# A fused retention and MLP kernel: half products in the second block, another order of plain units, and k scaled on GpSimd by a product

## The chip, the core and the metric

The kernel runs on one core of a Trainium2 chip. The metric is the device time in microseconds of one execution. The time before is the median of three runs, 205.53 us (205.35 to 206.09).

## What is computed

The reference is a retention layer (a decaying linear attention) over 4 batches, 8 heads, 768 tokens and a head size of 64, and behind it an MLP with a Mish-like gate over the 3072 tokens:

```python
gamma = 1.0 - 2.0 ** (-5.0 - np.arange(H))
for t in range(S):
    state = gamma * state + outer(k[t], v[t])
    y[t] = (1 / sqrt(D)) * q[t] @ state
x = y as (3072 tokens, 512)
h = x @ w_in                       # 512 -> 2048
g = h * tanh(log1p(exp(h)))        # Mish
out = g @ w_out                    # 2048 -> 512
```

Inputs and output are float32; the kernel multiplies in float16.

## The kernel before

The 3072 tokens are 24 chunks of 128, six to a batch. Chunks go in blocks: block 0 has four, blocks 1 to 10 two each. For each chunk q, k and v are loaded (a DMA each on SyncE's queue), scaled and cast to float16 (`casts`, L313 to L327), q and k are transposed by a DMA (`turn_by_dma`, L329) or on TensorE (`turn`, L354, for chunks 4 and 5), and then come the scores (L371), the mask (L377, VectorE), the state update (L385; su on VectorE at L397, st on GpSimd or VectorE at L398), y (L404 and L414) and the copy of y to xt (L460, ScalarE). In `casts` GpSimd makes three operations a chunk from chunk 6 on: q times a column of factors for each head (L319), k times one constant (L324, `tensor_scalar`), and v times a column of factors (L325). For chunks up to 5 ScalarE scales k (L322).

Everything is put in order by hand: the scheduler is manual, each engine works through its instructions in the order in which the program issues them, and each waits on semaphores for its inputs and for tiles to come free. For the first two blocks that order stands in `plan` dictionaries keyed by a unit number u; for the later blocks it stands in `steps_of`, keyed by step names ("p2", "p6", "p7", "p4", "h2", "end" in the first GEMM, "m2", "m7", "m3" in the second).

The two GEMMs of the MLP come in two forms:
- Plain. In blocks 0 and 1 `g1` (L468) makes the first GEMM: each unit fills one PSUM tile with matmuls against `win` (L475), and `mish` follows on ScalarE (L491). `g2_mm` (L495, L497) makes the second GEMM, 16 matmuls of 512 columns a chunk, and `g2_out` (L501) copies the result on VectorE (L503).
- With half products, from block 2 (`SEVEN = 2`). Matrices are cut in 2 x 2, and a product of two such matrices takes seven block products in place of eight, with sums of the inputs made beforehand and sums of the outputs behind. `g1_seven` (L578) does it for one half of the first GEMM's outputs: seven block products of eight 128-column matmuls (L600), with snapshots of PSUM on ScalarE (`snap`, L607) and sums on VectorE (`plus`, L617); the other half is made in four `plain` units of eight 256-column matmuls each (L620, L624, mish at L628). `seven` (L670) does it for the whole second GEMM: seven products of eight 256-column matmuls (L690), in the order a11 b11, a12 b21, s2 t2, s1 t1, s3 t3, s4 b22, a22 t4.

The sums that they need: `win_sums` (L546, written wsum, L562) and `weight_sums` (L511, written tmat, L527 to L530) once; `x_sums` (L569, xsum) of a block's xt before its first GEMM; and for the second GEMM sums of g in `gsum`: s1 and s2 by `sums_a` (L540, rows L543 and L544), s3 by `sums_b` (L664), s4 by `sums_c` (L668). All of them are VectorE operations on float16 tiles in SBUF. s1 is a21 + a22 and s2 is s1 - a11, so s2 of some f needs g of the units that made these f in all of those quarters. The 16 row blocks of g lie as f 0 to 7 in the first half and f 0 to 7 in the second; f 0 to 3 come from the half products, f 4 and 5 from `plain(1, 0)` and `plain(3, 0)`, f 6 and 7 from `plain(1, 1)` and `plain(3, 1)`.

Before the change the plain units stand in the order (1,0), (1,1), (3,0), (3,1), and `sums_a` is called twice, for f 0 to 3 at step "p7" and for f 4 to 7 at "end", behind the first mask of "h2". In block 1, the plain form, the eight tmat sums are issued one a unit (`extra`).

Of the kernel before, what the change touches and what calls it, by code (L numbers as in the profile page):

```python
# [9 lines left out]
FP16 = mybir.dt.float16  # L10
FP32 = mybir.dt.float32
AF = mybir.ActivationFunctionType
ALU = mybir.AluOpType
# [3 lines left out]
def kernel(  # L17
# [9 lines left out]
    nc = tc.nc  # L27
    B, H, S, D = q.shape
    d_model, d_ff = moe_w_in.shape
    P = 128  # L30
# [4 lines left out]
    TB = 512  # L35
    CPB = TB // C
# [4 lines left out]
    NFB = d_ff // P  # L41
    NBP = d_model // P
    NSL = 4
    FPS = NFB // NSL
# [36 lines left out]
    ident = cpool.tile([P, P], FP16, name="ident")  # L81
    tri = cpool.tile([P, C], FP32, name="tri")
    gcm = cpool.tile([P, HP, P], FP32, name="gcm")
    warm = cpool.tile([P, 1], FP32, name="warm")
    nc.gpsimd.memset(ident, 0.0)
    nc.gpsimd.affine_select(
# [17 lines left out]
    for h in range(H):  # L104
        o = 64 * (h % 2)
        nc.vector.memset(gcm[o:o + 64, h // 2, o:o + 64], float(gamma[h] ** C))

    win_ap = moe_w_in.rearrange("(bp p) f -> p bp f", p=P)
    wout_ap = moe_w_out.rearrange("(fb p) c -> p fb c", p=P)
# [5 lines left out]
    gtiles, tmats, gsums = {}, [], []  # L115
    wsums, hsnaps, tsums = [], [], {}
    nsnap = [0]
    SEVEN = 2
    nload, ncast = [0], [0]
    stores = []  # L120


# [190 lines left out]
    def casts(g):  # L313
        qf, kf, vf = loaded.pop(g)
        qk16 = castp.tile([P, 2, H, D], FP16, name="qk16")
        q16, k16 = qk16[:, 0], qk16[:, 1]
        v16 = castp.tile([P, H, D], FP16, name="v16")
        if qf is not None:
            nc.gpsimd.tensor_tensor(  # L319
                q16, qf, qs.unsqueeze(2).broadcast_to((P, H, D)), op=ALU.mult)  # L320
        if g < CPB + 2:
            nc.scalar.mul(k16, kf, BOOST)  # L322
        else:
            nc.gpsimd.tensor_scalar(k16, kf, BOOST, None, op0=ALU.mult)  # L324
        nc.gpsimd.tensor_tensor(  # L325
            v16, vf, vs.unsqueeze(2).broadcast_to((P, H, D)), op=ALU.mult)
        cast[g] = (q16, k16, v16, qk16)  # L327
# [170 lines left out]
            o_ps, gts[blk, fb][:, t * P:(t + 1) * P], wouts[s][:, f, cols],  # L498
            start=(fb == 0), stop=(fb == NFB - 1))

    def g2_out(o_ps, blk, t, due, cols=slice(None)):  # L501
        osb = op.tile(list(o_ps.shape), FP32, name="osb", tag="osb")
        nc.vector.tensor_copy(osb, o_ps)  # L503
        row0 = (first[blk] + t) * P
        dst = out[row0:row0 + P, cols]
        stores.append((due, dst, osb))
# [4 lines left out]
    def weight_sums(half):  # L511
        n, hf = NFB // 2, d_model // 2
        if half == 0:
            tmats.extend(
                wstage.tile([P, 2, n, hf], FP16, name="tmat", tag="wt", bufs=4)
                for _ in range(2))
            gsums.append(wstage.tile([P, 4, n, P], FP16, name="gsum", tag="wt", bufs=4))
            gsums.append(gp.tile([P, 4, n, P], FP16, name="gsum", tag="g0"))
            hsnaps.append(gp.tile([P, 4, TB], FP32, name="hsnap", tag="g0"))
        f = slice(half * FPS, (half + 1) * FPS)  # L520
        t1, t2 = tmats[0][:, 0, f], tmats[0][:, 1, f]
        t3, t4 = tmats[1][:, 0, f], tmats[1][:, 1, f]
        b11, b12 = wouts[half][:, :, :hf], wouts[half][:, :, hf:]
        b21, b22 = wouts[half + 2][:, :, :hf], wouts[half + 2][:, :, hf:]
        sub = ALU.subtract
        return [
            lambda: nc.vector.tensor_tensor(t1, b12, b11, op=sub),  # L527
            lambda: nc.vector.tensor_tensor(t2, b22, t1, op=sub),
            lambda: nc.vector.tensor_tensor(t3, b22, b12, op=sub),
            lambda: nc.vector.tensor_tensor(t4, b21, t2, op=sub),  # L530
        ]

    def sum_views(blk, f=slice(None)):
        s = gsums[blk % 2]
        n = NFB // 2
        lo, hi = gtiles[blk, 0][:, :n][:, f], gtiles[blk, 0][:, n:][:, f]
        return ([s[:, i, f] for i in range(4)],
                lo[:, :, :P], hi[:, :, :P], lo[:, :, P:], hi[:, :, P:])

    def sums_a(blk, half):  # L540
        n = NFB // 4
        (s1, s2, _, _), a11, _, a21, a22 = sum_views(blk, slice(half * n, (half + 1) * n))
        nc.vector.tensor_tensor(s1, a21, a22, op=ALU.add)  # L543
        nc.vector.tensor_tensor(s2, s1, a11, op=ALU.subtract)  # L544

# [32 lines left out]
    def g1_seven(blk, steps):  # L578
# [41 lines left out]
        def plain(s, half):  # L620
            h_ps = mmps.tile([P, 2, 2 * P], FP32, name="h_ps", tag="mm")
            for j in range(2):
                for bp in range(NBP):
                    nc.tensor.matmul(  # L624
                        h_ps[:, j], win(s, 2 * half + j, bp), xt(blk, bp),
                        start=bp == 0, stop=bp == NBP - 1)
            fb = s * FPS + 2 * half
            nc.scalar.activation(gt[:, fb:fb + 2], h_ps, AF.Mish, scale=inv_boost3)  # L628
# [21 lines left out]
        mish_of(1, 1, c22)  # L650
        mish_of(0, 1, c12)
        step("p7")
        plain(1, 1)
        mm(px, a(1, 1), t(4))
        mish_of(1, 0, px)
        step("p4")
        plain(3, 0)
        step("h2")
        plain(3, 1)
        step("end")  # L660
# [105 lines left out]
    def first_block():  # L766
# [85 lines left out]
            31: [(y_two, 1)],  # L852
        }
        o_tiles = [None] * CPB
        extra = []
        for u in range(2, 2 * NFB):
            if u < NFB:
                g1(0, u)
            elif u < 2 * NFB - 2:
                w = u - NFB  # L860
                for t in range(CPB):
                    if w == 0:
                        o_tiles[t] = mmps.tile([P, d_model], FP32, name="o_ps", tag="mm")
                    g2_mm(o_tiles[t], 0, t, w)
            else:
                for t in range(CPB // 2) if u % 2 == 0 else range(CPB // 2, CPB):
                    for w in range(NFB - 2, NFB):
                        g2_mm(o_tiles[t], 0, t, w)
                    g2_out(o_tiles[t], 0, t, 1)
            for fn, *args in plan.get(u + 1, ()):  # L870
                fn(*args)
            if u == NFB + 1:
                extra = win_sums()
            if extra:
                extra.pop(0)()

    def next_chunk(g):
        if g < NCK:
# [11 lines left out]
    def state_next(blk, j):  # L890
        if not last_of_batch(first[blk] + j):
            state(first[blk] + j, nc.gpsimd)

    def steps_of(blk):
        a, nb = first[blk] + 4, blk + 1
        ahead = nb < len(BLOCKS)

        def only(*work):
            return list(work) if ahead else []
        return {  # L900
            "p2": only((outer_next, nb), (state_next, nb, 0)),
            "p6": [(cast_to, a + 1), (next_chunk, a), (store_due, 1)],
            "p7": [(store_due, 2), *only((state_next, nb, 1)), (sums_a, blk, 0)],
            "p4": [(store_due, 3)],
            "h2": only((scores, a - 2), (scores, a - 1), (mask, a - 2)),
            "end": [(sums_a, blk, 1), (cast_to, a + 2), (next_chunk, a + 1)],
            "m2": only((mask, a - 1)),
            "m7": only((y_two, nb)),
            "m3": only((x_sums, nb)),
        }  # L910

    def plan_of(blk):
        a = first[blk] + 4
        early, then_seven = blk == 1, blk + 1 == SEVEN
        plan = {1: [(cast_to, a + 1)],
                (1 if early else 2 if then_seven else 4): [(cast_to, a + 1), (next_chunk, a)],
                (5 if early else 8): [(cast_to, a + 2), (next_chunk, a + 1)]}
        plan[10 if early else 7] = [(scores_two, blk + 1)]
        plan[12 if early else 10] = [(outer_two, blk + 1)]
        plan[14 if early else 13] = [(y_two, blk + 1)]  # L920
        return plan

    first_block()
    for blk in range(1, len(BLOCKS)):
        if blk >= SEVEN:
            steps = steps_of(blk)
            g1_seven(blk, steps)
            seven(blk, steps, blk + 1 == len(BLOCKS))
            continue
        n1 = NFB * BLOCKS[blk] // CPB  # L930
        plan = plan_of(blk)
        extra = []
        if blk + 1 == SEVEN:
            extra = weight_sums(0) + weight_sums(1)
        for u in range(2 * n1):
            store_due(u)
            if u < n1:
                g1(blk, u)
            else:
                t, part = divmod(u - n1, 4)  # L940
                if part == 0:
                    o_ps = mmps.tile([P, d_model], FP32, name="o_ps", tag="mm")
                for fb in range(part * 4, part * 4 + 4):
                    g2_mm(o_ps, blk, t, fb)
                if part == 3:
                    g2_out(o_ps, blk, t, u + 3 if t == 0 else 3)
            for fn, *args in plan.get(u, ()):
                fn(*args)
            if extra:
                extra.pop(0)()  # L950
        if blk + 1 == SEVEN:
            x_sums(SEVEN)
    store_due(2 * NFB)


# [28 lines left out]
```

## Time and profile before

| what | value |
|---|---|
| median of the runs | 205.53 us |
| the profiled execution, whole | 205.6 us |
| its span, first to last instruction | 203.8 us |
| TensorE busy | 195.1 us, granted clock 1.000 |
| VectorE / ScalarE / GpSimd busy | 146.9 / 99.8 / 93.9 us |
| L319, q on GpSimd, 20 of them | 23.4 us, 1172 ns each |
| L324, k on GpSimd, 18 of them | 27.7 us, 1540 ns each |
| L325, v on GpSimd, 20 of them | 21.8 us, 1089 ns each |
| block 1's first GEMM (64 matmuls of 256 columns) | 50.78 to 57.76 |
| starts of blocks 2 to 10 | 66.97, 82.71, 97.50, 112.43, 127.89, 142.68, 157.60, 173.06, 187.85 |

In the profile PE is TensorE, DVE VectorE, ACT ScalarE, POOL GpSimd, SP SyncE. A row of a timeline has the start and the length in us, the engine, the line of the kernel, the operation, the tiles written and read, the shapes, and a count where like instructions are merged; in brackets stands how long the engine had been idle and what ended that. Matmuls follow one another in a pipeline, so their starts tell more than their ends: 0.0558 us apart at 128 columns, 0.1092 at 256. Idle time of an engine that isn't the bottleneck costs nothing by itself.

### The profile page before, as it was taken

Reading aid. Unit: us, or ns where it says so; the run is one execution under the profiler, and the core shown is the slowest. Engines: PE = TensorE matmul, PEld = TensorE weight load, DVE = VectorE, ACT = ScalarE, POOL = GpSimd, SP = SyncE. Lnnn points to the kernel's source line nnn. Section 1 sums busy time; section 2 is a strip of 40 time slices with the busy share of each in tenths; the row PEclk is TensorE's granted clock in tenths of the full one; section 3 lists DMA queues with packets and bytes.
Section 4 is the critical chain, followed back from the end, with each engine's and each line's share of the span. In section 5 each row is a group of like instructions: output and inputs, shape, how many; then the busy total and the mean of one; then the engine's idle time right before and its main releaser. Section 6 shows DMA issues by size and latency. Waiting matters only on the chain.

```text
span 203.8 us, 5296 instructions
## 1 busy us (share of the span) xinstructions
PE 195.1 (96%) x2215; PEld 152.5 (75%) x2215; DVE 146.9 (72%) x247; ACT 99.8 (49%) x177; POOL 93.9 (46%) x85
## 2 busy tenths in 40 slices
PE   6897999999999999999999999999999999999993
PEld 2455544455865887988988988988988978988982
DVE  2677643868989688677697687777897687686552
ACT  2363664151530672673573563563653753753850
POOL 4072000609975396296473495498282593200000
PEclk9999999999999999999999999999999999999999
DMA  5999999997999989949999659939999452200202
GB/s 170 302 314 361 385 387 286 287 240 166 205 241 271 232 195 235 175 33 240 228 186 247 109 61 271 189 72 274 200 258 168 67 154 55 105 3 16 90 26 77
DMA packets 95895, 38.64 MB, mean 190 GB/s; under 512 B 82304, under 2 KB 89984, under 8 KB 95872
## 3 DMA queue, kind: packets, MB, share of 16 engines
q1 hardware_dynamic: 92608, 37.50, 80.6%
q10 hardware_dynamic: 3264, 0.82, 2.1%
q8 instruction: 17, 0.28, 0.6%
q14 instruction: 6, 0.05, 0.1%
HBM read 27.30 MB, written 6.29 MB: 165 GB/s over the span
## 4 chain that ended last, share of the span: by engine, by line
PE 85%; DVE 7%; ACT 3%; DMA 2%; issue 1%; DVEq 0%
PE o_ps L690 25%; PE h_ps L624 16%; PE h_ps L600 14%; PE h_ps L475 9%; PE o_ps L497 8%; PE at L371 3%; PE y_ps L414 3%; DMA qfirst<-in_q_dram 2%; PE y_ps L404 2%; DVE gsum L544 2%; PE u_ps L385 2%; DVE am L377 1%; PE h_ps L762 1%; ACT xt L460 1%; DVE gsum L543 1%
## 5 line engine op out<-in xcount | busy, mean ns | idle before, releaser
L624 PE MATMUL h_ps<-xt,win 128*128 128x256 f16 x288 | 37.3, 273 | 0.0
L319 POOL TENSOR_TENSOR qk<-qf,qvs 128x512 f16<-128x512 f32 x20 | 23.4, 1172 | 23.3 <-DMA qf<-in_q_dram 23.3
L398 POOL TENSOR_TENSOR st<-su,gcm 128x512 f16<-128x512 f32 x11 | 14.4, 1307 | 42.3 <-DVE su L397 42.3
L690 PEld LDWEIGHTS <-gsum 128*128 128x128 f16 x288 | 27.0, 98 | 6.1 <-DVE gsum L544 2.3
L624 PEld LDWEIGHTS <-win 128*128 128x128 f16 x288 | 26.4, 98 | 3.3
L324 POOL TENSOR_SCALAR qk<-kf 128x512 f16<-128x512 f32 x18 | 27.7, 1540 | 1.5
L690 PE MATMUL o_ps<-tmat,gsum 128*128 128x256 f16 x216 | 25.8, 273 | 1.0 <-DVE gsum L544 1.0
L617 DVE TENSOR_TENSOR hsum<-h_ps,hsnap 128x512 f32<-128x512 f32 x27 | 17.8, 687 | 12.4 <-PE h_ps L600 10.7
L377 DVE TENSOR_TENSOR am<-at,tri 128x1024 f16<-128x1024 f32 x20 | 24.2, 1217 | 1.2 <-PE at L371 1.0
L325 POOL TENSOR_TENSOR v<-vf,qvs 128x512 f16<-128x512 f32 x20 | 21.8, 1089 | 6.3 <-PE u_ps L385 4.8
L628 ACT ACTIVATE g<-h_ps 128x512 f16<-128x512 f32 x36 | 21.4, 593 | 5.6 <-PE h_ps L624 5.5
L607 ACT COPY hsnap<-h_ps 128x512 f32<-128x512 f32 x27 | 14.9, 587 | 17.0 <-PE h_ps L600 17.0
L690 PEld LDWEIGHTS <-g 128*128 128x128 f16 x216 | 21.1, 98 | 2.5
L497 PE MATMUL o_ps<-wout,g 128*128 128x512 f16 x96 | 22.7, 380 | 0.0
L460 ACT CAST xt<-y_ps 128x1024 f16<-128x1024 f32 x10 | 10.1, 1012 | 24.0 <-PE y_ps L414 16.6
L696 ACT COPY snap<-o_ps 128x256 f32<-128x256 f32 x27 | 10.0, 372 | 21.1 <-PE o_ps L690 21.1
L704 DVE TENSOR_TENSOR osb<-o_ps,snap 128x256 f32<-128x256 f32 x27 | 11.3, 419 | 12.0 <-PE o_ps L690 10.4
L475 PE MATMUL h_ps<-xt,win 128*128 128x256 f16 (+1 forms) x120 | 19.4, 322 | 0.1
L611 ACT ACTIVATE g<-hsum 128x512 f16<-128x512 f32 x27 | 16.8, 635 | 4.3 <-DVE hsum L617 4.3
L491 ACT ACTIVATE g<-h_ps 128x512 f16<-128x512 f32 x24 | 14.2, 597 | 8.4 <-PE h_ps L475 6.9
L600 PEld LDWEIGHTS <-wsum 128*128 128x128 f16 x288 | 17.2, 98 | 0.7
L475 PEld LDWEIGHTS <-win 128*128 128x128 f16 x120 | 11.7, 97 | 7.8 <-issue 0.4
(94 smaller groups left out, 295.7 us busy)
## 6 DMA issues: line engine op xcount, KB each, us to landing
kf<-in_k_dram SPq DMA_DIRECT2D x23, 256.0 KB, 4.7
vf<-in_v_dram SPq DMA_DIRECT2D x23, 256.0 KB, 5.1
out_dram<-osb SPq DMA_DIRECT2D x22, 256.0 KB, 3.7
qf<-in_q_dram SPq DMA_DIRECT2D x19, 256.0 KB, 4.1
wt<-in_moe_w_out_dram SPq DMA_DIRECT2D x3, 1024.0 KB, 8.7
wi<-in_moe_w_in_dram SPq DMA_DIRECT2D x4, 512.0 KB, 7.4
wi<-in_moe_w_in_dram SPq DMA_DIRECT2D x2, 1024.0 KB, 11.4
qfirst<-in_q_dram SPq DMA_DIRECT2D x2, 512.0 KB, 5.4
```

What stands on the lines that cost most here:

```text
L319: nc.gpsimd.tensor_tensor(q16, qf, qs.unsqueeze(2).broadcast_to((P, H, D)), op=ALU.mult)
L324: nc.gpsimd.tensor_scalar(k16, kf, BOOST, None, op0=ALU.mult)
L325: nc.gpsimd.tensor_tensor(v16, vf, vs.unsqueeze(2).broadcast_to((P, H, D)), op=ALU.mult)
L377: nc.vector.tensor_tensor(am, ats.pop(g), tri.unsqueeze(1).unsqueeze(1).broadcast_to((P, 2, HP, C)), op=ALU.mult)
L475: nc.tensor.matmul(h_ps[:, j], win(s, f, bp), xt(blk, bp), start=(bp == 0), stop=(bp == NBP - 1))
L497: nc.tensor.matmul(o_ps, gts[blk, fb][:, t * P:(t + 1) * P], wouts[s][:, f, cols], start=(fb == 0), stop=(fb == NFB - 1))
L600: nc.tensor.matmul(h_ps[:, f], w(f, d), x(d), start=first and f == 0 and d == 0, stop=d == n - 1, skip_group_check=True)
L611: nc.scalar.activation(gt[:, 2 * i * FPS:(2 * i + 1) * FPS, j * P:(j + 1) * P], h, AF.Mish, scale=inv_boost3)
L617: nc.vector.tensor_tensor(h, h_ps, x, op=ALU.add)
L624: nc.tensor.matmul(h_ps[:, j], win(s, 2 * half + j, bp), xt(blk, bp), start=bp == 0, stop=bp == NBP - 1)
L628: nc.scalar.activation(gt[:, fb:fb + 2], h_ps, AF.Mish, scale=inv_boost3)
L690: nc.tensor.matmul(o_ps, x(f), w(f), start=first and f == 0, stop=f == n - 1, skip_group_check=True)
```

## The change

- The k operation of `casts` on GpSimd becomes a product with `ks`, a tile of the constant, one column a head, broadcast over the head size, in the form of the q and v products.
- In `g1_seven` the units `plain(3, 0)` and `plain(1, 1)` change places.
- `sums_a` takes a slice of f and is called three times: f 0 to 3 at "p7", f 4 and 5 at "p4", f 6 and 7 at "end". The mask of "h2" now stands between the second and the third.
- Block 1 makes its first GEMM by `g1_seven`, with its own steps (`steps_of_half`) and its own `x_sums` at the end of block 0; its second GEMM stays plain.
- The wsum operations are issued two a unit, in four units of block 0, and two tmat sums follow there; the other six go into block 1 at "p6", "p7", "p4" and into two units of its second GEMM.
- The last of block 0's four output copies goes to ScalarE.
- Tiles for sums and snapshots are allocated at other places. The casts, loads and transposes of block 1 hang on step names in place of unit numbers; the order of the instructions on GpSimd and SyncE stays as it was.

```diff
+    ks = cpool.tile([P, H], FP32, name="ks")
+    nc.vector.memset(ks, BOOST)
-            nc.gpsimd.tensor_scalar(k16, kf, BOOST, None, op0=ALU.mult)
+            nc.gpsimd.tensor_tensor(
+                k16, kf, ks.unsqueeze(2).broadcast_to((P, H, D)), op=ALU.mult)
...
+    def g2_out(o_ps, blk, t, due, cols=slice(None), on_act=False):
         osb = op.tile(list(o_ps.shape), FP32, name="osb", tag="osb")
-        nc.vector.tensor_copy(osb, o_ps)
+        if on_act:
+            nc.scalar.copy(osb, o_ps)
+        else:
+            nc.vector.tensor_copy(osb, o_ps)
...
-    def sums_a(blk, half):
-        n = NFB // 4
-        (s1, s2, _, _), a11, _, a21, a22 = sum_views(blk, slice(half * n, (half + 1) * n))
+    def sums_a(blk, f):
+        (s1, s2, _, _), a11, _, a21, a22 = sum_views(blk, f)
         nc.vector.tensor_tensor(s1, a21, a22, op=ALU.add)
         nc.vector.tensor_tensor(s2, s1, a11, op=ALU.subtract)
...
         step("p7")
-        plain(1, 1)
+        plain(3, 0)
         mm(px, a(1, 1), t(4))
         mish_of(1, 0, px)
         step("p4")
-        plain(3, 0)
+        plain(1, 1)
         step("h2")
         plain(3, 1)
         step("end")
...
-                    g2_out(o_tiles[t], 0, t, 1)
+                    g2_out(o_tiles[t], 0, t, 1, on_act=t == CPB - 1)
...
             if u == NFB + 1:
-                extra = win_sums()
-            if extra:
-                extra.pop(0)()
+                late.extend(win_sums())
+            if NFB < u <= NFB + 4:
+                late.pop(0)()
+                late.pop(0)()
+            if u == NFB + 4:
+                late.extend(weight_sums(0))
+            if u in (NFB + 5, NFB + 8):
+                late.pop(0)()
...
+    def some_late(n):
+        for _ in range(min(n, len(late))):
+            late.pop(0)()
+
+    def steps_of_half(blk):
+        a = first[blk] + 4
+        return {
+            "p6": [(store_due, 1), (cast_to, a + 1), (next_chunk, a), (some_late, 1)],
+            "p7": [(store_due, 3), (some_late, 1)],
+            "p4": [(some_late, 2)],
+            "h2": [(cast_to, a + 2), (next_chunk, a + 1)],
+        }
...
-            "p7": [(store_due, 2), *only((state_next, nb, 1)), (sums_a, blk, 0)],
-            "p4": [(store_due, 3)],
+            "p7": [(store_due, 2), *only((state_next, nb, 1)),
+                   (sums_a, blk, slice(0, FPS))],
+            "p4": [(store_due, 3), (sums_a, blk, slice(FPS, FPS + 2))],
             "h2": only((scores, a - 2), (scores, a - 1), (mask, a - 2)),
-            "end": [(sums_a, blk, 1), (cast_to, a + 2), (next_chunk, a + 1)],
+            "end": [(sums_a, blk, slice(FPS + 2, 2 * FPS)), (cast_to, a + 2), (next_chunk, a + 1)],
...
     first_block()
+    x_sums(HALF_SEVEN)
+    late.extend(weight_sums(1))
+    room_for_sums()
     for blk in range(1, len(BLOCKS)):
...
+        g1_seven(blk, steps_of_half(blk))
...
-            if u < n1:
-                g1(blk, u)
...
+            some_late(1)
+        x_sums(blk + 1)
```

More of the change, by code (lines that the diff above doesn't have):

```diff
@@ L117 @@
     nsnap = [0]
-    SEVEN = 2
-    nload, ncast = [0], [0]
+    SEVEN, HALF_SEVEN = 2, 1
+    nload, ncast, late = [0], [0], []
     stores = []
@@ L499, in g2_mm @@
             start=(fb == 0), stop=(fb == NFB - 1))
-    def g2_out(o_ps, blk, t, due, cols=slice(None)):
+    def g2_out(o_ps, blk, t, due, cols=slice(None), on_act=False):
         osb = op.tile(list(o_ps.shape), FP32, name="osb", tag="osb")
-        nc.vector.tensor_copy(osb, o_ps)
+        if on_act:
+            nc.scalar.copy(osb, o_ps)
+        else:
+            nc.vector.tensor_copy(osb, o_ps)
         row0 = (first[blk] + t) * P
@@ L516, in weight_sums @@
                 for _ in range(2))
-            gsums.append(wstage.tile([P, 4, n, P], FP16, name="gsum", tag="wt", bufs=4))
-            gsums.append(gp.tile([P, 4, n, P], FP16, name="gsum", tag="g0"))
-            hsnaps.append(gp.tile([P, 4, TB], FP32, name="hsnap", tag="g0"))
         f = slice(half * FPS, (half + 1) * FPS)
@@ L531, in weight_sums, with room_for_sums @@
         ]
+    def room_for_sums():
+        n = NFB // 2
+        gsums.append(wstage.tile([P, 4, n, P], FP16, name="gsum", tag="wt", bufs=4))
+        gsums.append(gp.tile([P, 4, n, P], FP16, name="gsum", tag="g0"))
     def sum_views(blk, f=slice(None)):
@@ L854, in first_block @@
         o_tiles = [None] * CPB
-        extra = []
         for u in range(2, 2 * NFB):
@@ L872, in first_block @@
             if u == NFB + 1:
-                extra = win_sums()
-            if extra:
-                extra.pop(0)()
+                late.extend(win_sums())
[6 more added lines that the diff above has]
+                late.pop(0)()
+        hsnaps.append(gp.tile([P, 4, TB], FP32, name="hsnap", tag="g0"))
     def next_chunk(g):
@@ L912, in plan_of @@
     def plan_of(blk):
[L913 to L921, printed above, removed]
+        return {10: [(scores_two, blk + 1)], 12: [(outer_two, blk + 1)], 14: [(y_two, blk + 1)]}
     first_block()
+    x_sums(HALF_SEVEN)
+    late.extend(weight_sums(1))
+    room_for_sums()
     for blk in range(1, len(BLOCKS)):
@@ L929 @@
             continue
+        g1_seven(blk, steps_of_half(blk))
         n1 = NFB * BLOCKS[blk] // CPB
         plan = plan_of(blk)
[L932 to L935, printed above, removed]
+        for u in range(n1, 2 * n1):
             store_due(u)
-            if u < n1:
-                g1(blk, u)
[L939 to L946, printed above, removed]
+            t, part = divmod(u - n1, 4)
+            if part == 0:
+                o_ps = mmps.tile([P, d_model], FP32, name="o_ps", tag="mm")
+            for fb in range(part * 4, part * 4 + 4):
+                g2_mm(o_ps, blk, t, fb)
+            if part == 3:
+                g2_out(o_ps, blk, t, u + 3 if t == 0 else 3)
             for fn, *args in plan.get(u, ()):
                 fn(*args)
[L949 to L952, printed above, removed]
+            some_late(1)
+        x_sums(blk + 1)
     store_due(2 * NFB)
```

## Prediction

> **What bounds the kernel now.** The page's first part comes first: TensorE is busy for almost the whole span, so what counts is TensorE's own work and the few moments in which it stands still.
>
> ```profile
> PE 195.1 (96%) x2215; PEld 152.5 (75%) x2215; DVE 146.9 (72%) x247; ACT 99.8 (49%) x177; POOL 93.9 (46%) x85
> ```
>
> The table of waits, asked for TensorE, names one wait after the opening:
>
> ```profile
> PE o_ps L690 <- DVE gsum L544: 1.0, 3, 0.4
> ```
>
> TensorE waits for VectorE's sums of g. By the starts of the matmuls it is a little more: 0.61, 0.43 and 0.43 us in blocks 2, 5 and 8, and 0.12 in blocks 4 and 7, 1.71 us together. Why VectorE is late there is read from three timelines of block 5; TensorE's, VectorE's, GpSimd's:
>
> ```profile
> 119.17 1.05 PE L624 MATMUL h_ps<-xt,win 128*128 128x256 f16 x8
> 120.05 1.91 PE L690 MATMUL o_ps<-wout,g 128*128 128x256 f16 x16
> 121.80 0.60 PE L690 MATMUL o_ps<-tmat,gsum 128*128 128x256 f16 x4
> 122.66 2.36 PE L690 MATMUL o_ps<-tmat,gsum 128*128 128x256 f16 x20 [0.27 <-DVE gsum L544]
> ```
> ```profile
> 118.13 0.42 DVE L543 TENSOR_TENSOR gsum<-g 128x512 f16<-128x512 f16 x1
> 118.59 0.42 DVE L544 TENSOR_TENSOR gsum<-gsum,g 128x512 f16<-128x512 f16 x1
> 119.05 1.23 DVE L377 TENSOR_TENSOR am<-at,tri 128x1024 f16<-128x1024 f32 x1
> 120.88 0.55 DVE L543 TENSOR_TENSOR gsum<-g 128x512 f16<-128x512 f16 x1 [0.60 <-ACT g L628]
> 121.46 1.15 DVE L544 TENSOR_TENSOR gsum<-gsum,g 128x512 f16<-128x512 f16 x1
> ```
> ```profile
> 114.90 1.27 POOL L398 TENSOR_TENSOR st<-su,gcm 128x512 f16<-128x512 f32 x1 [6.02 <-DVE su L397]
> 116.13 1.04 POOL L319 TENSOR_TENSOR qk<-qf,qvs 128x512 f16<-128x512 f32 x1
> 117.26 1.49 POOL L324 TENSOR_SCALAR qk<-kf 128x512 f16<-128x512 f32 x1
> 118.82 1.09 POOL L325 TENSOR_TENSOR v<-vf,qvs 128x512 f16<-128x512 f32 x1
> 119.88 1.26 POOL L398 TENSOR_TENSOR st<-su,gcm 128x512 f16<-128x512 f32 x1
> 121.11 1.22 POOL L319 TENSOR_TENSOR qk<-qf,qvs 128x512 f16<-128x512 f32 x1
> 122.41 1.54 POOL L324 TENSOR_SCALAR qk<-kf 128x512 f16<-128x512 f32 x1
> 124.03 1.04 POOL L325 TENSOR_TENSOR v<-vf,qvs 128x512 f16<-128x512 f32 x1
> ```
>
> Read the last two together. One and the same sum takes 0.42 us under the old k operation (118.13, under L324) and 1.15 us when it meets a GpSimd product (121.46, under L319, which ends at 122.33; the sum ends 0.28 later). The first late sum ends 0.28 after L398 too (121.42 against 121.14). The wsum, tmat and xsum rows do the same under L319 and L325: a VectorE operation with two inputs in SBUF stands until the GpSimd product is over, gets in, and the next product then starts some 0.2 late. In the 14 such places that I counted VectorE came in as soon as the product ended, and in all five where both had more waiting, GpSimd came next: they alternate. Under L324 the sums run on; only within about 0.4 us of its start are they held (the sums_b row at 122.53 takes 1.09 for 0.68). Masks (1.23 under L325 and L398) and hsums read one input from PSUM and aren't held.
>
> **The k product.** 18 operations of 1540 ns become products of the form of L325 (1089 ns mean, 1.04 alone): I take 1.05 us, since shape, types and broadcast are those of L325. GpSimd saves 18 x 0.45 = 8 us of busy time, and it bounds nothing. What is lost is the gap in which sums could run: each cast becomes three products in a row that hold VectorE, and there are two casts in each of blocks 2 to 8. [...]
>
> **Sums in three parts, plain units in another order.** The order on VectorE becomes: s1, s2 over four f; s1, s2 over f 4 and 5; the mask; s1, s2 over f 6 and 7. Two more held operations stand ahead of the mask. TensorE needs the last pair later than before: at f = 6 of the third product, 22 matmuls after the first of the second GEMM, not 20. In block 5 that is 120.05 + 22 x 0.1092 = 122.45. Now the alternation, with 1.05 a product, 1.25 for st, and a held sum ending 0.28 (512 columns) or 0.15 (256; the xsum at 142.71 ended 0.14 after L325) behind the product:
> - k 117.2 to 118.25; s1 ends 118.55; v 118.5 to 119.55; s2 ends 119.83.
> - st 119.8 to 121.05; s1(4,5) ends 121.2; q to 122.25; s2(4,5) ends 122.4.
> - k 122.4 to 123.45 beside the mask, 122.4 to 123.6; v from 123.5 to 124.55; s1(6,7) ends 124.7; s2(6,7) 125.0.
>
> TensorE waits 125.05 - 122.45 = 2.6 us for 0.43 now: **+2.15** in blocks 2, 5, 8 (two st on GpSimd). In blocks 3 and 6 the first sum starts under k and all of v, q, k fall between the sums: in block 6 the sums end 133.95, 135.23, 136.4, 137.6, the mask 138.8, the last pair 139.4; needed at 135.28 + 2.40 = 137.68: **+1.7**. In blocks 4 and 7 the st, q, k come between: in block 7 the sums end 148.8, 150.2, 151.35, 152.55, the mask 153.75, the last pair 154.25; needed at 150.30 + 2.40 = 152.70, 1.55 for 0.12: **+1.4**. Blocks 9 and 10 have no casts: 0. TensorE has no slack to win any of it back. Sum 3 x 2.15 + 2 x 1.7 + 2 x 1.4 = **12.7 us**. The sums behind (s3, s4, mask, xsum) find GpSimd done in this picture, except where the next chunk's q lands just then (139.34 in block 6): up to 1.4 us more in each of blocks 3 and 6.
>
> **Block 1 by half products.** 64 matmuls x 0.1092 = 6.99 us become 56 of 128 columns (0.0558 each by their starts) and 32 x 0.1092, 6.62: -0.36. Added on VectorE: four xsums (0.28) and three hsums (0.69); on ScalarE three snaps (0.59), whose engine was idle 0.28 us before each mish. GpSimd casts chunks 6 to 8 all through this stretch, so the xsums are held: the second, by k and v products of 1.05 us each, ends near 53.8, while TensorE wants it 1.35 us after the block's start at 51.9: 0.65 lost. The rest (c11, c22, slots) I find just in time. Net **+0.3**; bounds -0.36 and +1.8 (c11 behind all four xsums, each held once more).
>
> **The end of the first block.** The wsums go out two to a unit, and two tmat sums follow. In the trace the sixth wsum ends at 39.97 as a q product starts (39.90 to 40.94); the seventh, now right behind it, is held to 41.2, the eighth ends 41.6, tmat (0.68) 42.3, and the qkt copy (41.11 now) comes behind them, 42.3 to 42.95. TensorE's scores, at 41.87 with nothing to spare, start at about 42.95: **+1.1**; without the meeting +0.3. The second tmat fits in the 0.72 us that VectorE idles before the second copy. The osb copy on ScalarE (nearest row L607, 0.59) lies in 1.12 us of idle time: 0. The memset of ks lies ahead of the first data: 0. GpSimd's and SyncE's instructions keep their order; the k products end sooner, so the transposes start sooner, and nothing waits for them: 0.
>
> **Sum.** 12.7 + 0.3 + 1.1 = 14.1. The profiled run took 205.6 us (span 203.8 and 1.8 around it; the median is 205.53, the same): **219.7 us**. With one product fewer among the sums of each of seven blocks, 7 x 1.05 = 7.4 less, 212; with the next chunk's casts falling in and block 1 at its worst, 2 x 1.4 + 1.5 more, 223.5.
>
> **Rivals.**
> - [...] 0.18.
> - About half the price, 206.6 to 212, say 209: the alternation holds, but the moved phase lets two products of each block pass beside ScalarE waits and the mask (7 x 2.1 off at most). 0.16.
> - No change: gains and losses cancel, 204.6 to 206.6. 0.05.
> - [...] The rows of L325 leave it 0.03.
> - My forecast, 212 to 223.5: 0.58.
>
> A measurement of this kernel can tell some 0.5% from no change. Faster 0.18, same 0.05, slower 0.77. The range 204.0 to 223.5 leaves out most of the faster case and what lies above.
>
> **What would show it.** In the changed kernel: k rows of 1.05 us as TENSOR_TENSOR; sums of 0.4 us drawn to 1.1 to 1.3, each ending 0.15 to 0.3 behind a GpSimd product; TensorE's table with waits for gsum of 1.5 to 2.6 in blocks 2 to 8 and none in 9 and 10; a wait for qkt near 42; block 1's first GEMM in about 7.3 us. It is wrong if the sums of f 6 and 7 end before TensorE asks, or if they run on under the k product as they do under L324.

## The result and the profile after

The changed kernel takes 219.8 us (median; 218.3 to 222.2), the kernel before on the same chip 205.49: a ratio of 1.067 (95% interval 1.061 to 1.073). One run, at 222.15 us and a mean granted clock of 0.977, counts as slow and is left out of the ratio. The profiled execution took 219.71 us, its span 217.9 us against 203.8: 14.1 us more.

The first part of the page, and from its groups the k operation and the second sum of a pair (last columns: busy us, mean ns of one | idle us ahead of it):

```profile
PE 199.1 (91%) x2239; PEld 154.5 (71%) x2239; DVE 162.6 (75%) x272; ACT 101.6 (47%) x181; POOL 86.1 (39%) x85
...
L326 POOL TENSOR_TENSOR qk<-kf,ks 128x512 f16<-128x512 f32 x18 | 19.5, 1084 | 0.0
```

TensorE's share fell from 96% to 91%. VectorE has 15.7 us more busy time, though the added operations are few; GpSimd has 7.8 us less, and the k row fell from 1540 to 1084 ns. The k operation is cheaper and the kernel is longer. TensorE's table of waits (us in total, times, longest), with the lines that bear on the change:

```profile
PE o_ps L697 <- DVE gsum L551: 10.2, 9, 2.0
...
PE at L374 <- DVE qkt L365: 0.8, 1, 0.8
...
PE h_ps L607 <- DVE xsum L581: 0.4, 1, 0.4
```

The wait for gsum stood at 1.0 us before. Counted by the starts of the matmuls, as in all that follows, the waits for gsum are 2.12, 1.28, 1.33, 0.79 + 1.43, 1.22, 1.33 and 0.79 + 1.43 us in blocks 2 to 8, together 11.72 for 1.71 before: 10.0 us more, and none in blocks 9 and 10. Block 5 again, TensorE, VectorE and GpSimd:

```profile
126.69 0.60 PE L697 MATMUL o_ps<-tmat,gsum 128*128 128x256 f16 x4
127.91 0.39 PE L697 MATMUL o_ps<-tmat,gsum 128*128 128x256 f16 x2 [0.63 <-DVE gsum L551]
129.57 3.15 PE L697 MATMUL o_ps<-tmat,gsum 128*128 128x256 f16 x18 [1.27 <-DVE gsum L551]
```
```profile
123.02 1.33 DVE L550 TENSOR_TENSOR gsum<-g 128x512 f16<-128x512 f16 x1
124.38 1.37 DVE L551 TENSOR_TENSOR gsum<-gsum,g 128x512 f16<-128x512 f16 x1
125.68 1.13 DVE L550 TENSOR_TENSOR gsum<-g 128x256 f16<-128x256 f16 x1
126.84 1.01 DVE L551 TENSOR_TENSOR gsum<-gsum,g 128x256 f16<-128x256 f16 x1
127.78 1.21 DVE L380 TENSOR_TENSOR am<-at,tri 128x1024 f16<-128x1024 f32 x1
128.91 0.28 DVE L550 TENSOR_TENSOR gsum<-g 128x256 f16<-128x256 f16 x1
129.22 0.29 DVE L551 TENSOR_TENSOR gsum<-gsum,g 128x256 f16<-128x256 f16 x1
```
```profile
123.03 1.04 POOL L328 TENSOR_TENSOR v<-vf,qvs 128x512 f16<-128x512 f32 x1
124.03 1.45 POOL L401 TENSOR_TENSOR st<-su,gcm 128x512 f16<-128x512 f32 x1
125.44 1.22 POOL L321 TENSOR_TENSOR qk<-qf,qvs 128x512 f16<-128x512 f32 x1
126.62 1.09 POOL L326 TENSOR_TENSOR qk<-kf,ks 128x512 f16<-128x512 f32 x1
127.67 1.09 POOL L328 TENSOR_TENSOR v<-vf,qvs 128x512 f16<-128x512 f32 x1
```

Read VectorE against GpSimd: four sums in a row, each about as long as the product beside it, each ending 0.14 to 0.28 us behind that product, and one product to each sum. The four take 4.8 us, from 123.02 to 127.85, for some 1.4 us of work (0.42 alone at 512 columns, 0.28 at 256). The mask stands behind them and the last pair behind the mask; TensorE takes its 23rd matmul of the second GEMM up at 129.57.

The waits are not all. From the first matmul of block 5 to that of block 6 it took 15.45 us before and takes 18.86 now, 3.4 more, of which its waits explain 1.8; block 8 is the same. Here the view of windows tells the rest, in three stretches of 3.41 us of block 5 (busy us and count of PE, of PEld, which is TensorE's loading of weights, of DVE, ACT and POOL, then the granted clock, DMA share, GB/s):

```profile
127.12:130.53 3.41, 1.52 (x13) 0.99 (x12) 3.38 (x7) 0.37 (x1) 1.64 (x2) 1.00 1.21 272
130.53:133.94 3.41, 3.41 (x29) 2.62 (x29) 2.08 (x3) 0.37 (x1) 0.00 (x0) 0.50 1.23 245
133.94:137.35 3.41, 3.41 (x52) 3.13 (x49) 1.72 (x7) 1.60 (x2) 0.00 (x0) 1.00 0.84 138
```

In the first, TensorE stands still in two gaps, 2.2 us by the starts (the view's 1.52 busy leaves 1.9). In the second the granted clock is 0.50 and 29 matmuls go through where the third takes 52 (of other sizes in part); those of 256 columns start 0.2133 us apart in place of 0.1092. The same happens from 181.73 to 185.14 in block 8, 51.2 us later, fifteen such windows. These two windows cost about 1.6 us each, and they are the only ones with a half clock between the first matmuls and the last in the profiled execution. Two other runs of the kernel had a mean clock of 0.992 (219.88 and 218.31 us) where the profiled one had 0.984, so the number of such windows is not fixed.

Adding up: 10.0 waits for gsum, 3.2 clock, 0.9 at the end of block 0 and 0.2 in block 1, less 0.25 gained in the opening, make 14.05 of the 14.1 us. The gain in the opening is chance: a matmul of block 0 that starts at 34.21 us in the kernel before and at 33.97 here starts at 33.44 to 33.64 in three of the experiments below that leave the opening as it was before.

### The profile page after: what moved, and what is told of

It reads as the page before. It is cut to its first block, busy times and chain, and to the rows that moved or that the text cites. A ratio compares the mean times of both kernels' runs of the same rounds, so it can differ in the third digit from the quotient of the medians.

```text
span 217.9 us, 5374 instructions
## 1 busy us (share of the span) xinstructions
PE 199.1 (91%) x2239; PEld 154.5 (71%) x2239; DVE 162.6 (75%) x272; ACT 101.6 (47%) x181; POOL 86.1 (39%) x85
## 4 chain that ended last, share of the span: by engine, by line
PE 52%; DVE 26%; DMA 9%; SPq 5%; ACT 4%; issue 2%; DVEq 0%
PE o_ps L697 19%; PE h_ps L607 11%; DVE gsum L551 8%; PE h_ps L631 8%; DVE gsum L550 7%; PE o_ps L500 6%; DMA wi<-in_moe_w_in_dram 5%; DMA wt<-in_moe_w_out_dram 4%; ACT g L618 4%; DVE am L380 4%; SPq L218 3%; PE y_ps L417 3%; DVE wsum L569 2%; DVE hsum L624 2%; PE y_ps L407 2%
## 5 line engine op out<-in xcount | busy, mean ns | idle before, releaser
L631 PE MATMUL h_ps<-xt,win 128*128 128x256 f16 x320 | 41.2, 273 | 0.0
L697 PEld LDWEIGHTS <-gsum 128*128 128x128 f16 x288 | 27.5, 100 | 17.1 <-DVE gsum L551 12.7
L697 PE MATMUL o_ps<-tmat,gsum 128*128 128x256 f16 x216 | 28.5, 285 | 10.2 <-DVE gsum L551 10.2
L631 PEld LDWEIGHTS <-win 128*128 128x128 f16 x320 | 29.4, 98 | 3.6
L624 DVE TENSOR_TENSOR hsum<-h_ps,hsnap 128x512 f32<-128x512 f32 x30 | 19.8, 687 | 13.7 <-PE h_ps L607 11.7
L635 ACT ACTIVATE g<-h_ps 128x512 f16<-128x512 f32 x40 | 23.7, 593 | 5.6 <-PE h_ps L631 5.5
L711 DVE TENSOR_TENSOR osb<-o_ps,snap 128x256 f32<-128x256 f32 x27 | 11.4, 421 | 14.3 <-PE o_ps L697 11.2
L550 DVE TENSOR_TENSOR gsum<-g 128x256 f16<-128x256 f16 (+1 forms) x27 | 17.9, 664 | 4.2 <-ACT g L618 2.8
L551 DVE TENSOR_TENSOR gsum<-gsum,g 128x256 f16<-128x256 f16 (+1 forms) x27 | 20.1, 745 | 0.9
L607 PEld LDWEIGHTS <-wsum 128*128 128x128 f16 x320 | 19.1, 98 | 1.3 <-DVE xsum L581 0.6
L326 POOL TENSOR_TENSOR qk<-kf,ks 128x512 f16<-128x512 f32 x18 | 19.5, 1084 | 0.0
L697 PE MATMUL o_ps<-wout,g 128*128 128x256 f16 x144 | 17.2, 273 | 0.0
```

Of the source, the lines that this page charges most:

```text
L607: nc.tensor.matmul(h_ps[:, f], w(f, d), x(d), start=first and f == 0 and d == 0, stop=d == n - 1, skip_group_check=True)
L624: nc.vector.tensor_tensor(h, h_ps, x, op=ALU.add)
L631: nc.tensor.matmul(h_ps[:, j], win(s, 2 * half + j, bp), xt(blk, bp), start=bp == 0, stop=bp == NBP - 1)
L697: nc.tensor.matmul(o_ps, x(f), w(f), start=first and f == 0, stop=f == n - 1, skip_group_check=True)
```

## The experiments

**What holds a sum?** The theory at this point was: a VectorE sum (two SBUF inputs) stands for the whole of a GpSimd product and not for the whole of a `tensor_scalar`; the moved sums and the new product each cost waits. Rivals: any GpSimd operation holds, so the kind doesn't matter; or the new product alone is the cause. Four kernels take the two parts apart.

*The change without the k product:*

```diff
-            nc.gpsimd.tensor_tensor(
-                k16, kf, ks.unsqueeze(2).broadcast_to((P, H, D)), op=ALU.mult)
+            nc.gpsimd.tensor_scalar(k16, kf, BOOST, None, op0=ALU.mult)
```

> The changed kernel with only the k edit undone: k goes back to tensor_scalar on GpSimd, half products in block 1 and the three-part sums stay. Theory (a GpSimd product with two inputs holds VectorE's sums to its end and alternates with them, a tensor_scalar holds them only about 0.4 us): sums under the k rows run on at 0.3 to 0.45 us, but the pair over f 4 and 5 still meets v, st and q. Waits for gsum by the block 5 arithmetic: about +0.5 over the kernel before in blocks 2, 5, 8, +0.7 in 3 and 6, +1.6 in 4 and 7, 6.1 us, and about 1 us in blocks 0 and 1: 211 to 213.5 us, no drop of the granted clock. [...] Rival B (the k edit was the whole cost): 204 to 206 us.

Measured: 210.16 us, ratio 1.024 [1.022, 1.026]; waits for gsum 5.7 us in all, clock 1.00. The same block 5, VectorE and GpSimd:

```profile
119.97 0.42 DVE L547 TENSOR_TENSOR gsum<-g 128x512 f16<-128x512 f16 x1
120.42 0.42 DVE L548 TENSOR_TENSOR gsum<-gsum,g 128x512 f16<-128x512 f16 x1
120.77 1.13 DVE L547 TENSOR_TENSOR gsum<-g 128x256 f16<-128x256 f16 x1
121.93 1.24 DVE L548 TENSOR_TENSOR gsum<-gsum,g 128x256 f16<-128x256 f16 x1
```
```profile
119.09 1.49 POOL L324 TENSOR_SCALAR qk<-kf 128x512 f16<-128x512 f32 x1
120.66 1.09 POOL L325 TENSOR_TENSOR v<-vf,qvs 128x512 f16<-128x512 f32 x1
121.71 1.31 POOL L398 TENSOR_TENSOR st<-su,gcm 128x512 f16<-128x512 f32 x1
```

The first two sums run free beside the `tensor_scalar`, the next two stand behind v and st. Swapping one kind of operation for the other takes 9.6 us off, of which 6.0 are waits for gsum and 3.2 the clock. Both rivals fall: the kind matters, and the k product isn't the only cause. It came out 0.8 us below the expectation, since blocks 3 and 6 hardly wait (0.1 us, in block 6).

*The kernel before with the k product alone:*

```diff
-            nc.gpsimd.tensor_scalar(k16, kf, BOOST, None, op0=ALU.mult)
+            nc.gpsimd.tensor_tensor(
+                k16, kf, ks.unsqueeze(2).broadcast_to((P, H, D)), op=ALU.mult)
```

> The kernel before with only the k edit: k as a product on GpSimd, sums in two parts and plain units as before. Theory: the second pair of sums (f 4 to 7, one 1.2 us mask later) now meets q, k, v in a row; in block 6 it ends 138.9 against 137.46 needed (+1.4), in block 7 153.8 against 152.48 (+1.25), in blocks 2, 5, 8 +0.1 to +1.0; tmat sums of block 1 later by up to 0.5 on the path. 211 to 214.5 us. [...] Rival B (the three-part sums and the new order are the whole cost): 205 to 206.

Measured: 212.44 us, 1.035 [1.033, 1.037]; waits for gsum 9.1 us, up to 2.05 in one piece, clock 0.999. The time is as expected, its parts only in part: blocks 3, 4, 6 and 7 lost 1.0 to 1.1 us each, where I had 1.4 for block 6 and 1.25 for block 7, and blocks 5 and 8 lost 1.6 each where I had at most 1.0.

*The change with the old order of the plain units and two parts of sums:*

```diff
-        plain(3, 0)
+        plain(1, 1)
...
-        plain(1, 1)
+        plain(3, 0)
...
-            "p4": [(store_due, 3), (sums_a, blk, slice(FPS, FPS + 2))],
+            "p4": [(store_due, 3)],
-            "end": [(sums_a, blk, slice(FPS + 2, 2 * FPS)), (cast_to, a + 2), (next_chunk, a + 1)],
+            "end": [(sums_a, blk, slice(FPS, 2 * FPS)), (cast_to, a + 2), (next_chunk, a + 1)],
```

> The changed kernel with only the plain units and the sums put back: order (1,1) then (3,0), sums in two parts, k as a product, half products in block 1 kept. Theory: as the product of k alone, 211 to 214.5, plus the 0.9 us of the first block's qkt wait and about 0.2 us of block 1: 212 to 215.5. If the three-part sums in their new place cost nothing by themselves (Rival B of the k edit as the whole cost) it stays at 218 to 221.

Measured: 214.18 us, 1.042 [1.039, 1.045]; waits for gsum 9.25 us, clock 0.999. As expected.

*The kernel before with the new order and three parts alone* (the edit of the one above, the other way round):

> The kernel before with only the new order of plain units and the sums in three parts; k stays tensor_scalar and block 1 stays plain. Theory: waits for gsum as worked out for the changed kernel with tensor_scalar, 6.1 us more than before, none in blocks 0 and 1: 210.5 to 212.5. Rival (the reordering hides the sums as its smaller last part suggests, and only the product of k spoils it): 203.5 to 205.

Measured: 209.35 us, 1.020 [1.018, 1.022]; waits for gsum 5.5 us. It missed by 1.2 us on the low side: I had let blocks 2, 3 and 6 wait as well, but there enough of the sums fall beside the `tensor_scalar` (in block 6 the first three, 0.43, 0.42 and 0.28 us, under the row of k) for the last pair to be ready in time. No run takes the order of the plain units and the three parts apart.

**The rest of the change.** *Half products in block 1, and the weight sums and copy that go with them, without the other two parts* (the edits of the first and the third experiment together):

```diff
-            nc.gpsimd.tensor_tensor(
-                k16, kf, ks.unsqueeze(2).broadcast_to((P, H, D)), op=ALU.mult)
+            nc.gpsimd.tensor_scalar(k16, kf, BOOST, None, op0=ALU.mult)
...
-            "p4": [(store_due, 3), (sums_a, blk, slice(FPS, FPS + 2))],
+            "p4": [(store_due, 3)],
```

> The kernel before with only block 1 by half products (with what belongs to it: the wsums two a unit, the late tmats, one output copy on ScalarE); k stays tensor_scalar and the sums stay in two parts. Theory: -0.36 us of matmuls, at most 0.3 lost on an xsum, and 0.9 to 1.6 us on the qkt copy at the end of block 0, behind a held wsum and a tmat (the two kernels with the half products and the other edits lost 1.0 to 1.6 there): 205.8 to 206.8 us. Rival (the half products' saving holds and the first block's wait comes only with the other edits): 204.8 to 205.0.

Measured: 206.12 us against 205.07, 1.005 [1.004, 1.007]. Nearly all of it is one line of TensorE's waits (0.8 us by the table, 1.00 by the starts of the matmuls):

```profile
PE at L371 <- DVE qkt L362: 0.8, 1, 0.8
```

**The clock.** The theory: the two half-clock windows come from the empty time ahead of them and cost 3.3 us. The rival: they come from something else in the changed kernel, and stay when the gaps are filled. *The changed kernel with idle matmuls in the gaps, on a PSUM tile that is overwritten afterwards:*

```diff
+                for _ in range(fill.get(f, 0)):
+                    nc.tensor.matmul(
+                        pe, wouts[0][:, 0, :P], tmats[0][:, 0, 0], start=True, stop=True,
+                        skip_group_check=True)
...
-        mm(px, s(2), t(2))
+        mm(px, s(2), t(2), fill={2: {4: 0, 6: 16}, 5: {4: 5, 6: 10}, 8: {4: 5, 6: 10}}.get(blk, {6: 8} if blk < 8 else {}))
```

> The changed kernel with idle matmuls (a weight tile on a tmat tile into a PSUM tile that is overwritten afterwards) put where TensorE waits for gsum: 16 before f 6 in block 2, 5 before f 4 and 10 before f 6 in blocks 5 and 8, 8 before f 6 in blocks 3, 4, 6, 7, each 0.109 us and together shorter than each wait. Theory (the granted clock of 0.5 for 3.41 us after the waits of blocks 5 and 8 comes from TensorE's empty time there and costs 1.6 to 1.7 us each): the waits stay, the clock stays 1.0, 216 to 217 us. Rival (the lower clock has another cause, or no time is lost by it): 219 to 220 us as the changed kernel.

Measured: 216.4 us (215.3 to 217.5), 1.055 [1.052, 1.059], clock 0.999. Matmuls whose result nobody reads make the kernel 3.4 us faster than the change, because the clock stays up. Block 5 takes 17.26 us for 18.86 and block 8 17.25 for 18.86, 1.6 less each; blocks 2, 3, 4, 6 and 7 take as long as in the changed kernel to 0.01 us, so the sums were as late as before. So the empty time was what brought the clock down, and the size is right.

**Two ways out that failed.** *Before, with the product s1 t1 ahead of s2 t2*, so that the sums of g would have eight matmuls more to be ready:

```diff
+        mm(pe, s(1), t(1), True)
+        m5 = snap(pe)
         mm(px, s(2), t(2))
...
-        mm(pe, s(1), t(1), True)
-        m5 = snap(pe)
         mm(px, s(3), t(3))
```

> The kernel before with one edit that the change does not have: in the second GEMM the products s1 t1 and s2 t2 change places, so that s2 is needed 8 matmuls (0.87 us) later. Theory (1.71 us of waits for gsum are all that can be won, and the latest second sum ends 0.61 us behind its need): no wait for gsum is left, 203.4 to 204.0 us. Rival (the held sums, sums_b, masks and sums_c behind them, become late in turn): 204.6 to 205.5.

Measured: 209.77 us, 1.024 [1.022, 1.025]: missed by nearly 6 us. TensorE's table:

```profile
PE o_ps L690 <- ACT snap L696: 3.6, 7, 0.5
PE o_ps L690 <- DVE am L377: 1.0, 2, 0.5
```

The wait for gsum is gone, and one of 0.68 us (0.62 in block 2) stands in each of nine blocks in its place: s2 t2 and s3 t3 write one PSUM tile, px, and are now neighbours, so the second must wait for ScalarE's snapshot of the first (0.37 us and the hand-over). In two blocks the table names a mask, which ended 0.02 to 0.03 us behind the snapshot. The product between them had hidden that copy. *The same with the half products of block 1, the first two tmat sums moved behind the qkt copies:*

```diff
-            if u in (NFB + 5, NFB + 8):
+            if u in (NFB + 8, NFB + 10):
                 late.pop(0)()
```

> The swapped products together with block 1 by half products, the first two tmat sums moved behind the two qkt copies; k stays tensor_scalar, sums in two parts. Theory: 1.71 us of waits and 0.36 us of matmuls go, 0.0 to 0.4 us is lost on the held eighth wsum and an xsum: 203.0 to 203.8 us, the fastest so far. Rival (the half products bring VectorE work onto the path and cost as much as they save): 203.9 to 205.

Measured: 209.69 us, 1.023 [1.021, 1.024], missed for the same reason. It shows one thing more: the wait for qkt stays (0.99 us), though no tmat sum stands ahead of the copy; a held wsum is enough (here the seventh, 1.26 us).

**The hold by itself.** *A kernel of sums on VectorE and, beside them, products or `tensor_scalar` operations on GpSimd, in the shapes of this kernel:*

```python
def products(n):
    for _ in range(n):
        nc.gpsimd.tensor_tensor(
            pk, xf, ks.unsqueeze(2).broadcast_to((P, H, D)), op=ALU.mult)

def scalars(n):
    for _ in range(n):
        nc.gpsimd.tensor_scalar(pk, xf, 2.0, None, op0=ALU.mult)

def sums(n):
    for _ in range(n // 2):
        nc.vector.tensor_tensor(t, s, a, op=ALU.add)
        nc.vector.tensor_tensor(s, t, a, op=ALU.subtract)
```

> A kernel that leaves the whole computation out and measures the disputed cost by itself, on the shapes of this kernel: GpSimd products and tensor_scalar operations alone, VectorE sums (128 x 512 float16, two inputs in SBUF, each needing the one before) alone, sums beside 8 GpSimd products, sums beside 8 tensor_scalar operations, and masks (128 x 1024, one input in PSUM) beside 8 products. Theory: sums alone some 0.43 us; beside products 1.2 to 1.4 us each, one for one with the products; beside tensor_scalar 0.43 to 0.85; masks 1.2 us beside products as without. [...] Rival B (no hold, the long sums in the kernel have another cause): 0.43 us everywhere.

Measured, in one execution: as the theory expects. VectorE and GpSimd, sums beside eight products, then beside eight `tensor_scalar`:

```profile
26.72 1.15 DVE L61 TENSOR_TENSOR t<-s,a 128x512 f16<-128x512 f16 x1
27.91 1.15 DVE L62 TENSOR_TENSOR s<-t,a 128x512 f16<-128x512 f16 x1
...
35.91 0.86 DVE L62 TENSOR_TENSOR s<-t,a 128x512 f16<-128x512 f16 x1
36.80 0.43 DVE L61 TENSOR_TENSOR t<-s,a 128x512 f16<-128x512 f16 x1
37.27 0.42 DVE L62 TENSOR_TENSOR s<-t,a 128x512 f16<-128x512 f16 x1
37.73 0.71 DVE L61 TENSOR_TENSOR t<-s,a 128x512 f16<-128x512 f16 x1
```
```profile
25.37 9.31 POOL L52 TENSOR_TENSOR pk<-xf,ks 128x512 f16<-128x512 f32 x8
...
35.89 12.77 POOL L57 TENSOR_SCALAR pk<-xf 128x512 f16<-128x512 f32 x8
```

Eight products took 9.31 us and let exactly one sum through each (1.15 us, 1.18 apart; 0.42 alone). A `tensor_scalar` holds a sum only at its start, by 0.3 to 0.4 us, and the others took 0.42 to 0.43. Masks with an input in PSUM took 1.22 us beside products; in block 9 of the changed kernel, with GpSimd idle (at 194.01 and 196.94 us), they take 1.22 too. A product hardly waits for a sum: the eight started 1.18 us apart beside sums and 1.12 beside masks.

**What if GpSimd leaves k out altogether?** *The change with every k on ScalarE:*

```diff
-        if g < CPB + 2:
-            nc.scalar.mul(k16, kf, BOOST)
-        else:
-            nc.gpsimd.tensor_tensor(
-                k16, kf, ks.unsqueeze(2).broadcast_to((P, H, D)), op=ALU.mult)
+        nc.scalar.mul(k16, kf, BOOST)
```

> The changed kernel with the k product taken off GpSimd: ScalarE scales k for every chunk, as the kernel does for chunks up to 5. Theory (the loss is GpSimd's products standing between the sums): one product less in each row of three, so about the time with tensor_scalar on GpSimd, 208 to 211 us, and no clock of 0.5. Rival A (what costs is the moved sums and the half products alone, the kind of k operation is of no weight): 217 to 220. Rival B (ScalarE's 18 extra operations of 0.63 us hold up snapshots and mish): 212 or more with waits of TensorE for ScalarE.

Measured: 212.83 us, 1.037 [1.036, 1.039]: missed by nearly 2 us, and 2.7 slower than with the `tensor_scalar` on GpSimd. The time lies in the range of rival B, but its sign is missing: TensorE hardly waits for ScalarE (0.2 us), and the first sum starts 5.86 us into block 5, as in the changed kernel. TensorE waits for gsum, 8.4 us. Block 5, VectorE and GpSimd:

```profile
121.46 1.38 DVE L545 TENSOR_TENSOR gsum<-gsum,g 128x512 f16<-128x512 f16 x1
122.77 1.12 DVE L544 TENSOR_TENSOR gsum<-g 128x256 f16<-128x256 f16 x1
123.92 1.02 DVE L545 TENSOR_TENSOR gsum<-gsum,g 128x256 f16<-128x256 f16 x1
```
```profile
121.05 1.51 POOL L395 TENSOR_TENSOR st<-su,gcm 128x512 f16<-128x512 f32 x1
122.52 1.22 POOL L319 TENSOR_TENSOR qk<-qf,qvs 128x512 f16<-128x512 f32 x1
123.70 1.09 POOL L322 TENSOR_TENSOR v<-vf,qvs 128x512 f16<-128x512 f32 x1
```

Without k, the products st, q and v close up and stand beside the sums. The `tensor_scalar` was not a cost but the gap in which sums could run. What counts here is which products fall among the sums, not how many GpSimd has.

*Before, with the second state product of a block on VectorE*, to take one product out of that place:

```diff
-    def state_next(blk, j):
+    def state_next(blk, j, by=nc.gpsimd):
         if not last_of_batch(first[blk] + j):
-            state(first[blk] + j, nc.gpsimd)
+            state(first[blk] + j, by)
...
-            "p7": [(store_due, 2), *only((state_next, nb, 1)), (sums_a, blk, 0)],
+            "p7": [(store_due, 2), *only((state_next, nb, 1, nc.vector)), (sums_a, blk, 0)],
```

> The kernel before with one edit that the change does not have: the second st of a block (step p7) is made on VectorE in place of GpSimd, some 0.7 us there. Theory: in blocks 2, 5 and 8 GpSimd's second cast starts 1.3 us earlier, so its q product is over before the second pair of sums and the sums run beside tensor_scalar; in blocks 4 and 7 they meet no st. Waits for gsum fall from 1.7 to 0.0 to 0.5 us: 203.4 to 204.4 us. Rival (VectorE's extra 0.7 us, itself held by the v product, makes the mask and the sums as late as before): 204.8 to 206.

Measured: 205.06 us against 205.39, 0.998 [0.997, 0.9995]: the fastest of all, but by 0.2%, a fifth of what I hoped and hardly more than can be told. The expectation missed and the rival's range came out. The 0.69 us of st now lie on VectorE itself, and the sum behind it meets v (1.15 us); of the waits for gsum, 1.1 us stay of 1.7.

## Why the prediction was right, and where only its sum was

The mechanism of the waits stood as predicted, and most of its numbers. That the total was met to 0.1 us is luck: a term that was 2.7 us too large and a missing one of 3.2 us nearly cancelled, and 0.25 us of chance in the opening and 0.3 too much at blocks 0 and 1 took up the rest. The upper bound was added up wrongly: 219.7 + 2 x 1.4 + 1.5 is 224.0, not 223.5, which changes nothing here.

- **Products alternate with sums, one for one; the mask isn't held.** Right: 1.15 us a sum beside 1.10 us a product in the kernel made for it, and 1.22 us a mask. The old k operation holds a sum 0.3 to 0.4 us at its start only, as read from the trace of before.
- **The k product costs 1.05 us.** Right: 1084 ns. In the kernel made for it the operation with one input took 1513 ns and the one with two 1070; a k product much longer than the old operation, which had the chance of 0.03, shows in no run.
- **12.7 us of waits for gsum in blocks 2 to 8.** The direction, the blocks and the order of sizes were right; the term was mis-sized: 10.0 measured. Per block it was 1.5 to 1.8 for 2.15 in blocks 2, 5 and 8, 1.2 to 1.3 for 1.7 in 3 and 6, 1.2 for 1.4 in 4 and 7. In block 5 I let the last pair be held by v, to 125.0 in the time of before. In the run the first sum (123.02) was held instead, as v had begun just with it, and when the mask ended, v was over (128.76): the pair ran in 0.6 us. So the sums alternated as forecast, but in block 5 five of them met a product in the forecast and four in the run. In blocks 3, 4, 6 and 7 the last pair ran free behind the mask, as forecast, but the held sums of 256 columns ended 1.05 us apart, where I had 1.15 to 1.2. That the sums behind cost nothing held: no further wait for them shows.
- **No term for the clock.** Missing: 3.2 us. I let full-rate matmuls follow every gap. In blocks 5 and 8 the forecast itself had 2.6 us of standing still a block, and I didn't ask what TensorE does next. The filled gaps show the empty time as the cause and give the size, 1.6 us a block.
- **The end of the first block, +1.1.** 0.9, a wait of 0.98 us in TensorE's timeline where 0.1 stood before, by the mechanism named but one operation later: the seventh wsum got through and the eighth was held. VectorE's timeline there, the held wsum, the tmat sum and the qkt copy:

```profile
39.99 1.27 DVE L569 TENSOR_TENSOR wsum<-win,wsum 128x512 f16<-128x512 f16 x1
41.17 0.68 DVE L530 TENSOR_TENSOR tmat<-wout 128x1024 f16<-128x1024 f16 x1
41.77 0.68 DVE L365 COPY qkt<-t_ps 128x1024 f16<-128x1024 f16 x1
```

- **Block 1, +0.3.** 0.2: its first GEMM took 7.17 us for 6.98. A held xsum made TensorE wait 0.55 us, by the matmuls' starts, which was nearly the 0.65 of the forecast, and half products gained 0.36.
- **The rivals.** Faster (203.5: without the 1.71 us of waits for gsum and with the 0.36 of block 1) would have needed the last pair before TensorE's 23rd matmul (22 after the first); TensorE waited 1.2 us or more for it in every block from 2 to 8. Half the price (209) is near what the kernel without the k product takes, 210.16. In the changed kernel one product a block passed beside the mask (v, in block 2 k), not two.

The parts by themselves cost 7.2 (k product), 4.1 (sums) and 1.1 us (block 1), 12.3 together; all at once cost 14.3. The added waits for gsum are fewer together, 10.0, than apart, 7.4 + 3.8; what makes the whole dearer than its parts is the clock, which fell in none of the single edits. Only the whole change has two gaps like those of 0.79 and 1.43 us so close together; that this closeness is what counts is not shown.

## What to carry to other kernels

Before making an operation of GpSimd shorter, see what VectorE does beside it: a longer operation that leaves VectorE's sums alone (here 1513 ns, with sums at 0.43 us) can be worth more than a shorter one that holds them (1070 ns, with sums at 1.15), and the price shows in TensorE's waits, not in GpSimd's row. When a forecast leaves TensorE standing still for some us in a few places close together (here 2.2 us in two gaps, with a granted clock of 0.50 for the 3.41 us behind them), allow for a fall of its clock, and look at the granted clock in the stretches that follow. When an order of products looks arbitrary, check which copy it hides before changing it.

## What had not been expected of the hardware

- A one-input `tensor_scalar` on GpSimd took 1513 ns for 128x512 elements, a product with a broadcast column 1070, as means of the kernel made for it; and the slower one, but for its start, let VectorE's sums run at 0.43 us.
- TensorE's clock was halved for 3.41 us after a stretch of 3.41 us with 2.2 us empty in block 5, in two gaps of 0.79 and 1.43, and again in block 8, where 0.62 of the first gap and the whole of the second lie in the stretch ahead, 2.05 us. Equally long empty time in one piece had no such effect: in the kernel with the k product and the old order of sums, one wait of 2.05 us by the starts (the view's 1.52 busy leaves 1.9) lies in a stretch of 3.41 us, and the clock stayed up in it and in the next:

```profile
174.06:177.47 3.41, 1.52 (x14) 1.13 (x13) 3.38 (x5) 0.37 (x1) 1.87 (x2) 1.00 0.41 77
177.47:180.88 3.41, 3.41 (x47) 2.98 (x46) 1.97 (x4) 1.38 (x2) 0.00 (x0) 1.00 0.02 5
```

The wait of 2.12 us in block 2 of the changed kernel was followed by no half clock either: 1.00 from 75.92 to 82.74. In that execution the clock fell at 130.53, at 181.73 and, behind the last matmul, at 219.28 us, 51.20 and 37.55 us apart, which is 15.0 and 11.0 times 3.413. By an estimate from these distances, in steps of 3.413 back from 130.53, a boundary would lie at 79.33, with 1.35 us of that wait on one side and 0.77 on the other. TensorE wasn't idle ahead of the first two falls: the view counts 13 matmuls in each of those stretches. Which gaps bring the clock down, and which don't, stays open; no run here varied them one at a time.
